# Moving weight sums from TensorE to loops on VectorE in a decode layer, with w1 loaded first

## The chip, the cores and the metric

The kernel runs on one core of a Trainium2 chip. The metric is device time in microseconds (us) for one execution; smaller is better. The core has five engines that matter here: PE (TensorE, with its weight loads listed apart as PEld), DVE (VectorE), ACT (ScalarE), POOL (GpSimd) and SP (SyncE). Each engine runs its own instruction list in order and waits on semaphores for the others. SP issues nearly all transfers from HBM to the on-chip memory; 16 DMA engines carry them.

## The reference, cut to what matters

One token of width 512 passes through a layer norm, then through two parallel branches, and all is added up. Everything is 32-bit floating point.

```python
xn = _layernorm(x)                       # x: 512 numbers, eps 1e-5
q  = (xn @ wq)                           # wq: 512 x 4096, 32 query heads of 128
# 8 key/value heads, 65536 cached keys each; 4 query heads share one of them
scores = q . k * 128**-0.5
o  = softmax(scores) . v                 # 32 heads of 128
h  = max(xn @ w1, 0)                     # w1: 512 x 1792
y  = x + o.reshape(4096) @ wo + h @ w2   # wo: 4096 x 512, w2: 1792 x 512
```

The caches k and v are 256 MiB each. The four weights are 8 MiB (wq), 8 MiB (wo), 3.5 MiB (w1) and 3.5 MiB (w2).

## The kernel before, in words

Keys are taken in 32 steps (8 key/value heads, 4 steps each). A step loads 8 MiB of k into the buffer `ks` and 8 MiB of v into the buffer `vs`; each buffer is 64 KiB deep on all 128 partitions, so it holds 32 *slices* of 512 numbers per partition, and a slice is 256 KiB in all. There is one buffer of each kind, with no second copy. In the text a slice always means these 256 KiB; wq and wo are 32 slices each, w1 and w2 are 14 each.

Queue of transfers. SP issues, in this order: wq in two pieces of 4 and 28 slices into `vs` (`WQ`, L169), the first k load into `ks` (L170); then, once PE has read all of wq (L310), the first v load. After that the loop at L312 alternates: a v load when `v_free` says that the step before has used its v, a k load when `k_free` says that the scores have been formed from the old k. At the end come w1 and w2 into `ks` (L318, L319, after the last `k_free`) and wo in seven pieces into `vs` (`WO`, L321, after the last `v_free`).

Start. DVE and PE form the layer norm with two small matmuls (L202 to L222), spread xn out (L226 to L256), and PE multiplies wq slice by slice into four rows of PSUM (L277 to L285). DVE and PE turn the result around into `qall` (L287 to L289). POOL copies the current head's query to `qcur` (L328).

A step. PE forms the scores from `ks` (L344), DVE transposes them into `tr` (L376), the maximum is found with help of PE (L349 to L351), ACT takes the exponentials (L422), and PE multiplies with `vs` into `acc_o` (L360). DVE then adds the step to `acc` (L400 or L402) and with that frees `vs` (L398). After four steps DVE closes the head (L406 to L415) into `fin`, and POOL copies it into `fins` (L332, L334).

End. PE forms xn @ w1 (L443), DVE and PE turn it around (L460, L271, L469), the heads are turned around and spread out (L453 to L494, result `sw`). PE multiplies the 14 slices of w2 and the first 28 of wo into `acc_z` (L505, helper `gather`), DVE copies that row (L536), and PE adds it together with the last four slices of wo into `acc_y` (L525, L540). DVE transposes `acc_y` (L552), and SP writes y (L561).

The helper class `Flow` counts an engine's operations on one semaphore and emits a wait only where it was not waited for already. `nc.Fori(0, n, engines=[...])` is a loop that runs on the chip: the engines named hold a counter in a register, and each turn ends with an add and a branch on each of these engines. `bass.ds(t * D, D)` is a part of a buffer whose place depends on that counter.

Of the kernel before, what the change touches and what calls it, by code (L numbers as in the profile page):

```python
# [15 lines left out]
P = 128  # L16
# [9 lines left out]
CHUNK = SK  # L26
# [3 lines left out]
NP = TPC // NT  # L30
# [6 lines left out]
WQ = [4, 28]  # L37
WO = [8, 8, 8, 4, 2, 1, 1]
PAIRED = 16
DIRECT = 28  # L40
# [29 lines left out]
def attention_and_mlp_kernel(  # L70
# [35 lines left out]
    def bank(name, *shape):  # L106
        return nc.alloc_psum_tensor(name, [P, *shape], F32).ap()

    ks = place("ks", NT * KEYS)
    vs = place("vs", NT * KEYS)  # L110
    tr = place("tr", NT * SUB, 32)
    wt = place("wt", NT * SUB, G)
    xT, xc, sq, xn = (place(n, A) for n in ("xT", "xc", "sq", "xn"))
    x4, yt = place("x4", P), place("yt", 32, 4)
    sw = place("sw", SLICES)
    mine = place("mine", HKV)
    octet = place("octet", P)
    eighth = place("eighth", R)

    flat_tr = tr.rearrange("p b i -> p (b i)")  # L120
    xs = flat_tr[:, : SLICES * HKV].rearrange("p (i h) -> p i h", h=HKV)
    xm = flat_tr[:, SLICES * HKV : SLICES * (HKV + 1)]
    om, spread = flat_tr[:, : R * HQ], flat_tr[:, R * HQ : 2 * R * HQ].rearrange("p (r h g) -> p r h g", r=R, h=HKV)
    heads = flat_tr[:, 2 * R * HQ : 2 * R * HQ + 2 * DH]
    st = place("st", 8)
# [4 lines left out]
    qall, qcur = place("qall", HKV, G), place("qcur", 32)  # L130
# [7 lines left out]
    acc, masked = place("acc", WIDE, DH), place("masked", WIDE, DH)  # L138
    fin, fins = place("fin", DH + G), place("fins", HKV, DH + G)
    rows = place("rows", 512)  # L140
    total, oT, hT = place("total", HQ), place("oT", HQ), place("hT", 4 * CT)
# [4 lines left out]
    names = "k_in v_in tiles scores m_out bias_out a_out w_out o_out k_free v_free q_in d_out f_out f_free"  # L146
    (
        k_in, v_in, s_tiles, s_dve, s_max, s_bias, s_alpha, s_w, s_o,
        k_free, v_free, q_in, s_diff, f_out, f_free,
    ) = (nc.alloc_semaphore(n) for n in names.split())  # L150
    PE, DV, AC, GP = (Flow(nc, e, n) for e, n in ((te, "pe"), (ve, "dve"), (se, "act"), (ge, "pool")))
# [6 lines left out]

    def load_slices(name, src, counts):
        marks = []  # L160
        for n in counts:
            cut = slice(len(marks) * D, (len(marks) + n) * D)
            marks += [load(sy, f"{name}{len(marks)}", vs[:, cut], src[:, cut])] * n
# [11 lines left out]
    make_identity_marks = []  # L175

# [3 lines left out]
    d = memset(DV, ones, 1.0)  # L180
    d = memset(DV, x4, 0.0)
    x4_free = DV.mark
    d = memset(DV, qcur, 0.0)
    for t in (acc_o, acc_z, pm):
        memset(DV, t, 0.0)
    memset(DV, acc_y[:, :P], 0.0)

# [9 lines left out]
    x4_in = None  # L197
    se.wait_ge(*x4_free)
    x4_in = load(se, "x4_in", x4[0:P:32, :], x.rearrange("(c n) -> c n", c=CT))


    DV.op(lambda e: e.reduce_sum(st[:, 0:1], xT, axis=AX.X), x_in)  # L202
    PE.op(lambda e: e.matmul(pm[:, 0:1], ones, st[:, 0:1], start=True, stop=True), DV.mark)
    DV.op(lambda e: e.tensor_scalar_mul(st[:, 1:2], pm[:, 0:1], 1.0 / D), PE.mark)
    DV.op(lambda e: e.tensor_scalar(xc, xT, st[:, 1:2], None, op0=ALU.subtract), DV.mark)
    DV.op(lambda e: e.tensor_mul(sq, xc, xc), DV.mark)
    DV.op(lambda e: e.reduce_sum(st[:, 2:3], sq, axis=AX.X), DV.mark)
    PE.op(lambda e: e.matmul(pm[:, 1:2], ones, st[:, 2:3], start=True, stop=True), DV.mark)
    DV.op(
        lambda e: e.tensor_scalar(st[:, 3:4], pm[:, 1:2], 1.0 / D, EPS, op0=ALU.mult, op1=ALU.add),  # L210
        PE.mark,
    )
# [3 lines left out]
    AC.op(lambda e: e.activation(alpha[:, 0:1], st[:, 3:4], AF.Exp))  # L216
# [5 lines left out]
    xn_in = DV.op(lambda e: e.tensor_scalar_mul(xn, xc, st[:, 7:8]), DV.mark)  # L222
# [14 lines left out]
    DV.op(lambda e: e.reduce_sum(mine, ident.rearrange("p (h i) -> p h i", h=HKV), axis=AX.X))  # L237
    DV.op(lambda e: e.reduce_sum(eighth, ident.rearrange("p (i r) -> p r i", r=R), axis=AX.X))
    DV.op(lambda e: e.reduce_sum(octet[:, : P // R], ident.rearrange("p (i r) -> p i r", r=R), axis=AX.X))
    DV.op(  # L240
        lambda e: e.tensor_copy(
            octet[:, P // R :].rearrange("p (h i) -> p h i", i=P // R),
            octet[:, : P // R].unsqueeze(1).to_broadcast([P, HKV - 1, P // R]),
        ),
        DV.mark,
    )
    DV.op(
        lambda e: e.tensor_mul(
            xm.rearrange("p (r a) -> p r a", a=A),
            eighth.unsqueeze(2).to_broadcast([P, R, A]), xn.unsqueeze(1).to_broadcast([P, R, A]),  # L250
        )
    )
    pz = pb[:, 1, :]
    PE.op(lambda e: e.matmul(pz[:, :SLICES], octet, xm, start=True, stop=True), DV.mark)
    xs_in = DV.op(
        lambda e: e.tensor_mul(  # L256
            xs, pz[:, :SLICES].unsqueeze(2).to_broadcast([P, SLICES, HKV]),
            mine.unsqueeze(1).to_broadcast([P, SLICES, HKV]),
        ),
        PE.mark,  # L260
    )
    DV.op(lambda e: e.memset(idg, 1.0))
    DV.op(lambda e: e.tensor_copy(idg[:, :G], ident[:G, :G]), DV.mark)

    pr, pt = pa[:, 0, :], pb[:, 0, :]

    def turn():

        for j in range(4):
            PE.op(  # L270
                lambda e: e.transpose(pt[:, j * P : (j + 1) * P], rows[:, j * P : (j + 1) * P], ident),  # L271
                DV.mark, made,
            )
        return pt.rearrange("p (j c l) -> p j c l", j=4, c=CT)

    cleared = DV.op(lambda e: e.memset(pr, 0.0))
    for i in range(SLICES):  # L277
        c = i % CT
        PE.op(
            lambda e: e.matmul(  # L280
                pr[32 * c : 32 * c + HKV, :], xs[:, i, :], vs[:, i * 512 : (i + 1) * 512],
                start=(i < CT), stop=(i >= SLICES - CT),
            ),
            cleared, xs_in, wq_in[i],
        )  # L285
    wq_read = PE.mark
    DV.op(lambda e: e.tensor_copy(rows, pr), PE.mark)  # L287
    q = turn()[:, :, :, :HKV].rearrange("p j c h -> p h j c")
    DV.op(lambda e: e.reduce_sum(qall, q, axis=AX.X), PE.mark)  # L289
    q_made = DV.mark  # L290
    PE.need(DV.mark)
    AC.need(DV.mark)


    def k_load(h, n):
        sy.wait_ge(k_free, 1).then_inc(k_free, -1)
        sy.dma_start(ks, k[h, 0, :, n * NT * KEYS : (n + 1) * NT * KEYS]).then_inc(k_in, 16)

    def v_load(h, n):
        sy.wait_ge(v_free, 1).then_inc(v_free, -1)  # L300
        src = v[h].rearrange("(p t b) d -> p t (b d)", p=P, b=SUB)
        sy.dma_start(vs, src[:, n * NT : (n + 1) * NT, :].rearrange("p t f -> p (t f)")).then_inc(v_in, 16)

    def head(h):
        v_load(h, 0)
        for n in range(1, NP):
            k_load(h, n)
            v_load(h, n)

    sy.wait_ge(*wq_read)  # L310
# [6 lines left out]
    t1, t2 = ks[:, : A * DFF], ks[:, A * DFF : A * DFF + FB * D]  # L317
# [7 lines left out]
    for h in range(HKV):  # L325
        if h:
            ge.wait_ge(f_out, h)
        ge.tensor_copy(qcur[:, :G], qall[:, h, :]).then_inc(q_in, NP)  # L328
        if h == 0:
            ge.sem_inc(f_free, 1)  # L330
        else:
            ge.tensor_copy(fins[:, h - 1, :], fin).then_inc(f_free, 1)  # L332
    ge.wait_ge(f_out, HKV)
    GP.op(lambda e: e.tensor_copy(fins[:, HKV - 1, :], fin))  # L334


    with nc.Fori(0, STEPS, engines=[ENG.PE]):
# [20 lines left out]
        for i in range(n):  # L358
            c = i % CT
            mm = te.matmul(  # L360
                acc_o[32 * c : 32 * c + WIDE * G, :],
                wt[:, i * WIDE : (i + 1) * WIDE, :].rearrange("p b g -> p (b g)"),
                vs[:, i * 512 : (i + 1) * 512],
                start=(i < CT), stop=(i >= n - CT),
            )
# [52 lines left out]
    with nc.Fori(0, HKV, engines=[ENG.Activation]):  # L418
# [16 lines left out]
        ).then_inc(s_alpha, 1)  # L435


    w = t1.rearrange("p (a f) -> p a f", a=A)
    for a in range(A):
        for c in range(CT):  # L440
            lo, hi = 512 * c, min(DFF, 512 * (c + 1))
# [151 lines left out]
```

## Time and profile before

| what | value |
|---|---|
| median of 3 runs | 1303.16 us (1303.08 to 1303.2) |
| profiled execution, own time | 1303.26 us |
| its span, first to last instruction | 1301.9 us |
| moved from HBM | 560.99 MB, 431 GB/s over the span |
| DMA engines busy with the SP queue | 99.7% |
| PE, DVE, ACT, POOL busy | 664.9, 268.4, 76.0, 4.1 us |
| mean granted TensorE clock | 0.733 |

The profile lists instructions by source line, engine and operation, with destination and sources by the program's names. A timeline row begins with the start in us from the span's start and the duration in us. "Idle before" with a releaser tells how long the engine stood before an instruction and which engine's work, or which transfer, ended that. An engine's name with a q (SPq, DVEq) is its sequencer: DMA issues, register steps, branches, waits and drains, which don't count as busy. A row of the DMA section has the size of one transfer and the time from its issue to its landing.

### The profile page before, as it was taken

Reading aid. Unit: us, or ns where it says so; the run is one execution under the profiler, and the core shown is the slowest. Engines: PE = TensorE matmul, PEld = TensorE weight load, DVE = VectorE, ACT = ScalarE, POOL = GpSimd, SP = SyncE. Lnnn points to the kernel's source line nnn. Section 1 sums busy time; section 2 is a strip of 40 time slices with the busy share of each in tenths; the row PEclk is TensorE's granted clock in tenths of the full one; section 3 lists DMA queues with packets and bytes.
Section 4 is the critical chain, followed back from the end, with each engine's and each line's share of the span. In section 5 each row is a group of like instructions: output and inputs, shape, how many; then the busy total and the mean of one; then the engine's idle time right before and its main releaser. Section 6 shows DMA issues by size and latency. Waiting matters only on the chain. (4 is left out here: it accounts for less than half of the span.)

```text
span 1301.9 us, 10665 instructions
## 1 busy us (share of the span) xinstructions
PE 664.9 (51%) x4512; PEld 185.6 (14%) x4512; DVE 268.4 (21%) x398; ACT 76.0 (6%) x292; POOL 4.1 (0%) x22
## 2 busy tenths in 40 slices
PE   3355356455446445545545545544544644544658
PEld 1111111111111111111111111111111111111112
DVE  2221122221122222012222012222112222201222
ACT  0000000000000000000000000000000000000000
POOL 0000000000000000000000000000000000000000
PEclk9776676777677677667677677768777767767769
DMA  9999999999999999999999999999999999999998
GB/s 419 419 449 419 451 419 445 425 427 443 421 449 421 449 419 451 419 445 425 431 439 425 445 421 449 419 451 419 445 425 435 435 425 445 421 449 421 449 416 361
DMA packets 11101, 561.06 MB, mean 431 GB/s; under 512 B 1492, under 2 KB 1496, under 8 KB 1880
## 3 DMA queue, kind: packets, MB, share of 16 engines
q1 hardware_dynamic: 10944, 561.00, 99.7%
q8 instruction: 3, 0.05, 0.0%
q10 hardware_dynamic: 152, 0.00, 0.0%
q14 instruction: 2, 0.02, 0.0%
HBM read 560.99 MB, written 0.00 MB: 431 GB/s over the span
## 5 line engine op out<-in xcount | busy, mean ns | idle before, releaser
L360 PE MATMUL acc_o<-vs,wt 128*16 128x512 f32 x2048 | 296.3, 743 | 179.0 <-PEq L356 179.0
L344 PE MATMUL pa<-ks,qcur 128*32 128x512 f32 x1024 | 176.5, 822 | 323.8 <-PEq L339 323.8
L376 DVE STREAM_TRANSPOSE tr<-pa 128x1024 f32<-128x1024 f32 x64 | 80.0, 1250 | 412.9 <-PE pa L344 412.9
L344 PE MATMUL pb<-ks,qcur 128*32 128x512 f32 x1024 | 139.5, 665 | 0.0
L422 ACT ACTIVATE wt<-tr,bias 128x128 f32<-128x128 f32 x128 | 64.3, 511 | 1084.5 <-ACTq L420 1084.5
L360 PEld LDWEIGHTS acc_o<-vs,wt 128*16 128x16 f32 x2048 | 69.6, 114 | 379.0 <-issue 379.0
L344 PEld LDWEIGHTS pa<-ks,qcur 128*32 128x32 f32 x1024 | 38.9, 134 | 431.4 <-issue 422.4
L402 DVE SCALAR_TENSOR_TENSOR acc<-acc,alpha,acc_o 128x512 f32<-128x512 f32 x24 | 17.9, 747 | 353.2 <-PE acc_o L360 353.2
L376 DVE STREAM_TRANSPOSE tr<-pb 128x1024 f32<-128x1024 f32 x64 | 80.0, 1250 | 49.6 <-PE pb L344 49.6
L344 PEld LDWEIGHTS pb<-ks,qcur 128*32 128x32 f32 x1024 | 41.9, 132 | 107.8 <-issue 88.6
L349 PE MATMUL pm<-ident,m 128*4 128x128 f32 x32 | 10.3, 320 | 87.7 <-DVE m L388 67.2
L400 DVE COPY acc<-acc_o 128x512 f32<-128x512 f32 x8 | 5.5, 692 | 121.5 <-PE acc_o L360 121.5
L350 PE MATMUL pm<-dg,ones 4*128 4x4 f32 x64 | 15.4, 309 | 21.4 <-DVE dg L392 21.4
L385 DVE TENSOR_REDUCE mc<-tr 128x4 f32<-128x512 f32 x24 | 24.1, 1006 | 1.8
L422 ACT ACTIVATION_READ_ACCUMULATOR wt<-tr,bias 128x1 f32 x128 | 23.9, 187 | 0.0
L349 PEld LDWEIGHTS pm<-ident,m 128*4 128x4 f32 x32 | 2.6, 81 | 116.7 <-DVE m L388 89.0
L350 PEld LDWEIGHTS pm<-dg,ones 4*128 4x128 f32 x64 | 12.6, 245 | 29.0 <-DVE dg L392 29.0
L351 PE MATMUL pm<-dg,rowg 4*128 4x1 f32 x64 | 14.7, 296 | 0.0
L280 PE MATMUL pa<-vs,tr 128*8 128x512 f32 x64 | 9.6, 754 | 8.7 <-DMA vs<-wq 7.4
L351 PEld LDWEIGHTS pm<-dg,rowg 4*128 4x128 f32 x64 | 13.4, 258 | 0.0
L390 DVE TENSOR_REDUCE mg<-pm 4x1 f32<-4x128 f32 x32 | 8.9, 279 | 13.2 <-PE pm L349 13.2
L505 PE MATMUL acc_z<-vs,sw 128*1 128x512 f32 x56 | 10.1, 592 | 2.1 <-DMA vs<-wo 2.1
(98 smaller groups left out, 97.8 us busy)
## 6 DMA issues: line engine op xcount, KB each, us to landing
vs<-wq SPq DMA_DIRECT2D x1, 7168.0 KB, 21.3
ks<-w SPq DMA_DIRECT2D x2, 3584.0 KB, 22.4
vs<-wo SPq DMA_DIRECT2D x3, 2048.0 KB, 16.4
vs<-wq SPq DMA_DIRECT2D x1, 1024.0 KB, 4.8
vs<-wo SPq DMA_DIRECT2D x1, 1024.0 KB, 22.8
ks<-k SPq DMA_DIRECT2D x32, 28.8
vs<-v SPq DMA_DIRECT2D x32, 28.9
vs<-wo SPq DMA_DIRECT2D x1, 512.0 KB, 23.6
```

What stands on the lines that cost most here:

```text
L280: lambda e: e.matmul(pr[32 * c : 32 * c + HKV, :], xs[:, i, :], vs[:, i * 512 : (i + 1) * 512], start=(i < CT), stop=(i >= SLICES - CT),),
L344: i = te.matmul(tile_of[32 * c : 32 * c + 32, :], qcur, ks[:, at : at + TW], start=True, stop=True)
L349: te.transpose(pm[:G, :P], m, ident)._wait_ge(s_dve, 3).then_inc(s_max, 1)
L350: te.matmul(pm[:, P : P + G], ones[:G, :], dg[:, :G], start=True, stop=True)._wait_ge(s_dve, 4)
L351: te.matmul(pm[:, P + G : P + G + 1], rowg, dg[:, G : G + 1], start=True, stop=True).then_inc(s_max, 1)
L360: mm = te.matmul(acc_o[32 * c : 32 * c + WIDE * G, :], wt[:, i * WIDE : (i + 1) * WIDE, :].rearrange("p b g -> p (b g)"), vs[:, i * 512 : ...
L376: i = ve.transpose(tr[:, s * SUB : (s + 2) * SUB, :].rearrange("p b i -> p (b i)"), (pa, pb)[s // 2 % 2].rearrange("p i k -> p (i k)"),)._ ...
L385: i = ve.reduce_max(top, tr[:, :, :G].rearrange("p b g -> p g b"), axis=AX.X)
L390: ve.reduce_max(mg, pm[:G, :P], axis=AX.X)._wait_ge(s_max, 1)
L402: ve.scalar_tensor_tensor(flat, flat, alpha[:, n : n + 1], acc_o, op0=ALU.mult, op1=ALU.add)
L422: i = se.activation(wt[:, :, g], tr[:, :, g], AF.Exp, bias=bias[:, n, g : g + 1], scale=scale, accum_out=part[:, n, g : g + 1],)
L505: lambda e: e.matmul(acc_z[32 * c : 32 * c + 1, :], lhsT, row, start=c not in begun, stop=last),
```

## The change

Setup. The buffers `ks` and `vs` become halves of one buffer `kv`. x is loaded as 16 rows of 32 numbers, once instead of twice; the layer norm's two sums are formed on DVE with 32x32 transposes in place of two matmuls. SP issues w1 first, into `ks`, with a rearranged source: "(i h) a f -> h i (a f)", 8 groups of 16 rows, for the 128 partitions. wq follows in two halves of 16 slices. The first k load waits until DVE has read w1 (`w1_read`); the first v load waits for all 32 adds over wq (`q_dve`).

w1. DVE multiplies and adds its 4 pieces of 1792 (128 partitions each) into `h1`, PE sums over the partitions with 4 matmuls, DVE turns the result into 14 columns of `hs` and takes the maximum with 0. This lies ahead of wq's sum.

wq. A loop on DVE of 32 turns: each waits for its slice (`go_dve`, raised by POOL in two lots of 16), adds slice times a column of `xs` onto `accq`, and drains. One matmul and four small transposes then make the queries.

Main loop. As before, but the loops of DVE, ACT and POOL become one `Fori` over heads, SP's runs over steps, PE's branch gets a prefetch hint, and DVE's loop loses its `head_slot`. The arrays k and v are cut so that each load is one contiguous 8 MiB. The last v load goes in two pieces (21 and 11 slices), and PE waits for the second before its 22nd group.

End. w2 (two halves of 7 slices) and the first 16 slices of wo go into `ks` after the last `k_free`, the other 16 of wo after the last `v_free`. Over the first 34 of these 46 slices runs a loop of 17 turns: ACT scales an even slice in place and PE adds it up with a column of ones, DVE adds the odd slice onto `accy` and drains. Five further slices DVE adds alone, four go through PE to `acc_z`, DVE adds both sums into `rows`, and PE takes `rows` and the last three slices into `acc_y`. Transpose and store are as before, without the small loop around the transpose. TensorE's instruction list shrinks from 812 to 446.

```diff
-WQ = [4, 28]
-WO = [8, 8, 8, 4, 2, 1, 1]
-PAIRED = 16
-DIRECT = 28
+WO = [9, 7, 5, 4, 4, 1, 1, 1]
+DIRECT = 29
+LATE = 21 * D
+TURNS = 17
+ALONE = 5
...
-        x_in = load(se, "x_in", xT, x.rearrange("(p a) -> p a", p=P))
-        wq_in = load_slices("wq", wq.rearrange("h (i r) a f -> (h i) (r a f)", r=R), WQ)
-        sy.dma_start(ks, k[0, 0, :, : NT * KEYS]).then_inc(k_in, 16)
+        x_in = load(se, "x_in", x16, x.rearrange("(i s) -> i s", s=32))
+        w1_in = load(sy, "w1_in", t1, w1.rearrange("(i h) a f -> h i (a f)", h=HKV))
+        wq_in = load_slices("wq", vs, wq.rearrange("h (i r) a f -> (h i) (r a f)", r=R), [SLICES // 2, SLICES // 2])
...
+    for a in range(A):
+        w = t1[:, a * DFF : (a + 1) * DFF]
+        if a == 0:
+            DV.op(lambda e: e.tensor_scalar_mul(h1, w, xn[:, 0:1]), DV.mark, w1_in)
+        else:
+            DV.op(
+                lambda e: e.scalar_tensor_tensor(h1, w, xn[:, a : a + 1], h1, op0=ALU.mult, op1=ALU.add), DV.mark
+            )
+    w1_read = DV.mark
...
+    for n in range(2):
+        ge.wait_ge(*wq_in[n * SLICES // 2]).then_inc(go_dve, SLICES // 2)
+    DV.need(xs_in, hid_in, blank)
+    with nc.Fori(0, SLICES, engines=[ENG.DVE]) as t:
+        ve.wait_ge(go_dve, 1).then_inc(go_dve, -1)
+        ve.scalar_tensor_tensor(
+            accq, vs[:, bass.ds(t * D, D)], xs[:, bass.ds(t, 1)], accq, op0=ALU.mult, op1=ALU.add
+        ).then_inc(q_dve, 1)
+        ve.drain()
...
+    sy.wait_ge(*w1_read)
+    sy.sem_inc(v_late, 16 * (STEPS - 1))
+    sy.dma_start(ks, k_parts[0]).then_inc(k_in, 16)
+    sy.wait_ge(q_dve, SLICES)
     sy.sem_inc(v_free, 1)
-    with nc.Fori(0, HKV - 1, engines=[ENG.SP]) as h:
-        head(h)
-        k_load(h + 1, 0)
-    head(HKV - 1)
+    with nc.Fori(0, STEPS - 1, engines=[ENG.SP]) as i:
+        v_load(i)
+        k_load(i + 1)
+    sy.wait_ge(v_free, 1).then_inc(v_free, -1)
+    sy.dma_start(vs[:, :LATE], v_parts[STEPS - 1][:, :LATE]).then_inc(v_in, 16)
+    sy.dma_start(vs[:, LATE:], v_parts[STEPS - 1][:, LATE:]).then_inc(v_late, 16)
     sy.wait_ge(k_free, 1)
-    w1_in = load(sy, "w1_in", t1, w1.rearrange("p a f -> p (a f)"))
-    w2_in = load(sy, "w2_in", t2, w2.rearrange("p j n -> p (j n)"))
+    w2_in = load_slices("w2", t2, w2.rearrange("p j n -> p (j n)"), [FB // 2, FB // 2])
+    near = [n for i, n in enumerate(WO) if FB + sum(WO[: i + 1]) <= SLICES]
+    wo_in = load_slices("wo", wos, wo_of, near)
     sy.wait_ge(v_free, 1)
-    wo_in = load_slices("wo", wo.rearrange("h (i r) g f -> (h i) (r g f)", r=R), WO)
+    wo_in += load_slices("wo", wos, wo_of, WO[len(near) :], at=sum(near))
...
+    with nc.Fori(0, TURNS, engines=[ENG.Activation, ENG.PE, ENG.DVE]) as t:
+        even, odd = (kv[:, bass.ds((t * 2 + i) * D, D)] for i in range(2))
+        se.wait_ge(go_act, 1).then_inc(go_act, -1)
+        se.activation(even, even, AF.Copy, scale=hs[:, bass.ds(t * 2, 1)]).then_inc(go_pe, 1)
+        te.wait_ge(go_pe, 1).then_inc(go_pe, -1)
+        te.matmul(acc_z[:1], ones[:, 0:1], even, start=False, stop=False)
+        ve.wait_ge(go_dve, 1).then_inc(go_dve, -1)
+        ve.scalar_tensor_tensor(accy, odd, hs[:, bass.ds(t * 2 + 1, 1)], accy, op0=ALU.mult, op1=ALU.add)
+        ve.drain()
+    for j in range(gathered - CT, gathered):
+        c = (j + 1) % CT
+        PE.op(
+            lambda e: e.matmul(
+                acc_z[32 * c : 32 * c + 1], hs[:, j : j + 1], kv[:, j * D : (j + 1) * D], start=(c != 0), stop=True
+            ),
+            arrivals[j], sw_in,
+        )
+    z_in = PE.mark
+    for j in range(TURNS * 2, TURNS * 2 + ALONE):
+        ve.wait_ge(go_dve, j - TURNS * 2 + 1)
+        DV.op(
+            lambda e: e.scalar_tensor_tensor(
+                accy, kv[:, j * D : (j + 1) * D], hs[:, j : j + 1], accy, op0=ALU.mult, op1=ALU.add
+            ),
+            DV.mark,
+        )
+    folded = DV.op(lambda e: e.tensor_add(rows, accy, acc_z), z_in, DV.mark)
...
+    for j in range(DIRECT, SLICES):
+        if j == SLICES - 1:
+            direct(ones[:, 0:1], rows, folded)
+        direct(
+            hs[:, FB + j : FB + j + 1], wos[:, j * D : (j + 1) * D], sw_in, wo_in[j],
+            first=(j == DIRECT), last=(j == SLICES - 1),
+        )
```

More of the change, by code (lines that the diff above doesn't have):

```diff
@@ L29 @@
 NT = 8
-NP = TPC // NT
+NP = NCH
 STEPS = HKV * NP
@@ L207, in attention_and_mlp_kernel @@
[L207 to L212, printed above, removed]
+    memset(GP, accq, 0.0)
+    memset(GP, qall, 0.0)
+    memset(GP, accy, 0.0)
+    blank = GP.mark
+    memset(DV, ones, 1.0)
+    memset(DV, qcur, 0.0)
+    memset(DV, pm, 0.0)
+    half = R * 2
@@ new lines, in attention_and_mlp_kernel @@
+    for c in range(CT):
+        PE.op(
+            lambda e: e.matmul(pm[32 * c : 32 * c + 1, : 32 * FB], ones[:, 0:1], mlp[:, c], start=True, stop=True),
+            w1_read,
+        )
+    mlp_in = PE.mark
+    xs_in = DV.op(lambda e: e.tensor_copy(xs, x_of))
+    DV.op(lambda e: e.transpose(turned, pm[:, : 32 * FB]), mlp_in)
+    DV.op(
+        lambda e: e.tensor_scalar_max(hs[:, :FB], turned.rearrange("p (j l) -> p j l", l=32)[:, :, 0], 0.0), DV.mark
+    )
+    DV.op(
+        lambda e: e.tensor_mul(
+            rows[:half].rearrange("i (j s) -> i j s", s=32), x16.unsqueeze(1).to_broadcast([half, half, 32]),
+            ident[:half, :half].unsqueeze(2).to_broadcast([half, half, 32]),
+        ),
+    )
@@ new lines, in attention_and_mlp_kernel @@
+    for t in (acc_o, acc_z):
+        memset(DV, t, 0.0)
+    memset(DV, acc_y[:, :P], 0.0)
+    hid_in = DV.mark
+    for n in range(2):
[7 more added lines that the diff above has]
+        ve.drain()
@@ L333, in attention_and_mlp_kernel @@
[L333 to L337 removed]
+    ge.sem_inc(f_free, 1)
+    ge.tensor_copy(qcur[:, :G], qall[:, 0, :]).then_inc(q_in, NP)
+    with nc.Fori(0, STEPS, engines=[ENG.PE], hint_back_edge=True):
         te.wait_ge(k_in, 16).then_inc(k_in, -16)
@@ new lines, in attention_and_mlp_kernel, with direct @@
+    folded = DV.op(lambda e: e.tensor_add(rows, accy, acc_z), z_in, DV.mark)
+    def direct(lhsT, row, *marks, first=False, last=False):
+        for c in range(CT):
+            PE.op(
+                lambda e: e.matmul(
+                    acc_y[32 * c : 32 * c + 1, :P], lhsT, row[:, c * P : (c + 1) * P], start=first, stop=last
+                ),
+                *marks,
+            )
+    for j in range(DIRECT, SLICES):
[4 more added lines that the diff above has]
+            first=(j == DIRECT), last=(j == SLICES - 1),
+        )
@@ L492, in attention_and_mlp_kernel @@
     )
-    sw_in = DV.op(
-        lambda e: e.reduce_sum(
-            sw.rearrange("p (r g) -> p r g", r=R), spread.rearrange("p r h g -> p r g h"), axis=AX.X
-        ),
-        DV.mark,
-    )
-    begun = set()
-    def gather(c, lhsT, row, marks, last=False):
-        PE.op(
-            lambda e: e.matmul(acc_z[32 * c : 32 * c + 1, :], lhsT, row, start=c not in begun, stop=last),
-            *marks,
-        )
-        begun.add(c)
-    for c in range(CT):
-        own = slice(32 * c, 32 * c + 1)
-        PE.op(
-            lambda e, own=own: e.matmul(acc_y[own, :P], ones[own, 0:1], x4[own], start=True, stop=False),
-            x4_in,
-        )
```

340 lines of the change are left out of this document (134 added, 206 removed).

## The prediction

> **What bounds the kernel now.** I read the page's slices and DMA section first, then the timeline of both ends, then the groups.
>
> ```profile
> span 1301.9 us, 10665 instructions
> DMA  9999999999999999999999999999999999999998
> q1 hardware_dynamic: 10944, 561.00, 99.7%
> q8 instruction: 3, 0.05, 0.0%
> q10 hardware_dynamic: 152, 0.00, 0.0%
> vs<-wq SPq DMA_DIRECT2D x1, 7168.0 KB, 21.3
> vs<-wq SPq DMA_DIRECT2D x1, 1024.0 KB, 4.8
> vs<-v SPq DMA_DIRECT2D x32, 28.9
> ```
>
> The 16 DMA engines are busy from end to end with SP's queue. The time is the start of the first transfer, 561 MB at a fixed rate, and a short end. Nothing saves more than the two ends; anything that leaves the queue empty costs in full. The two wq rows give the pace: issued at 0.97 and 0.43 later (next fence), 4 slices land at 5.8 and 28 more at 22.7, so 16.9 / 28 = 0.604 us per slice, 19.3 us per 8 MiB. A transfer on an idle queue lands 4.8 - 4 x 0.604 = 2.4 us after its issue, plus its own length. In the steady state a v load lands 28.9 us after its issue, of which 19.3 is its own: each is issued 28.9 - 19.3 - 2.4 = 7 us before the queue would run dry. That is all the cover.
>
> ```profile
> 0.97 0.86 SPq L155 DMA_DIRECT2D vs<-wq  x2
> 13.49 1.89 PE L280 MATMUL pa<-vs,tr 128*8 128x512 f32 x8 [1.32 <-DVE pa L276]
> 22.80 7.74 PE L280 MATMUL pa<-vs,tr 128*8 128x512 f32 x56 [7.42 <-DMA vs<-wq]
> 31.11 0.35 SPq L302 DMA_DIRECT2D vs<-v  x1
> 42.51 2.79 PE L344 MATMUL pa<-ks,qcur 128*32 128x512 f32 x12 [10.42 <-PEq L339]
> ```
>
> At the start PE is done with wq at 22.80 + 7.74 = 30.5 and SP issues the first v load at 31.1 (0.57 later), while the first k load streams until about 42.3, where PE starts on it. So PE's sum over wq hides by 9 us.
>
> **The change, part by part.** *Start: w1 first.* w1's 14 slices move from the end to the start. In bytes this is neutral; the first k load would land at 42.3 + 14 x 0.604 = 50.8, and the first v load must be issued by 50.8 - 2.4 = 48.4 or the queue runs dry. On all 16 engines w1 lands at 1.0 + 2.4 + 8.5 = 11.9. But its source steps 8 groups of 16 rows, and no load of before does that. The nearest row is the ACT queue's 152 packets: the 128-row x load makes 128 + 16 completions, so the second one, of 4 rows, made only 8, 4 rows and 4 completions: it ran on 4 engines. If the outermost count sets the engines, w1 runs on 8, takes 17 us and lands at 20.3. Bounds 11.9 and 20.3; I take 20.3, as the row is for a small count too. [...]
>
> *DVE ahead of wq.* The layer norm stays under w1's transfer: before, it and the spreading of xn were over at 13.49, where PE starts on wq.
>
> ```profile
> L402 DVE SCALAR_TENSOR_TENSOR acc<-acc,alpha,acc_o 128x512 f32<-128x512 f32 x24 | 17.9, 747 | 353.2 <-PE acc_o L360 353.2
> L400 DVE COPY acc<-acc_o 128x512 f32<-128x512 f32 x8 | 5.5, 692 | 121.5 <-PE acc_o L360 121.5
> L409 DVE TENSOR_TENSOR masked<-acc,selb 128x512 f32<-128x512 f32 x8 | 5.5, 686 | 0.0
> L463 DVE COPY tr<-pb 128x256 f32<-128x256 f32 x1 | 0.4, 424 | 0.2 <-PE pm L458 0.2
> L376 DVE STREAM_TRANSPOSE tr<-pa 128x1024 f32<-128x1024 f32 x64 | 80.0, 1250 | 412.9 <-PE pa L344 412.9
> L178 DVE MEMSET acc_o<- 128x512 f32 x1 | 0.5, 485 | 0.1
> ```
>
> An element costs (692 - 424) / 256 = 1.05 ns, and 686 from on-chip memory beside 692 from PSUM says that the source hardly matters. So a multiply-add of 512 is 0.747, of 1792 it is 2.09; four are 8.4, and w1 is read at 28.7. Then four narrow matmuls (8 cold passes, 1.9), a transpose of 448 (0.7 between 0.41 and 1.25), a maximum (0.2), a 512-wide product (0.69) and three memsets (1.15): the wq loop starts at 33.4. SP's k load, behind `w1_read`, goes out at 29, before wq is through.
>
> *The wq loop.* The drain makes its turn serial.
>
> ```profile
> L406 DVEq DRAIN  x8: 650/652/652, 188.5 to 1273.0; - x8
> L370 DVEq COMPARE_BRANCH  x9: 100/129/143, 32.3 to 1274.8; - x9
> L370 DVEq ALU_OP  x8: 45/45/58, 190.2 to 1274.7; - x8
> L398 DVEq EVENT_SEMAPHORE  x32: 21/21/21, 72.2 to 1272.8; - x32
> L302 SPq FUSED_REGOPS  x7: 37/37/42, 30.9 to 962.8; - x7
> 1272.92 0.75 DVE L402 SCALAR_TENSOR_TENSOR acc<-acc,alpha,acc_o 128x512 f32<-128x512 f32 x1 [15.54 <-PE acc_o L360]
> 1273.74 0.17 DVE L408 TENSOR_TENSOR diff<-bias 128x12 f32<-128x12 f32 x1
> ```
>
> The L406 drain, issued behind the add at 1272.92, stands until the add is over: it lasts 0.65, and the next work starts at 1273.74, 0.07 after the add's end. Only then come counter (0.045), branch (0.129), the address steps that `bass.ds` needs (0.037 each on SP, one or two), the wait (0.021), and about 0.1 from the wait (1272.8) to the add (1272.92). Recorded durations alone: 0.747 + 0.07 + 0.045 + 0.129 + 0.021 + 0.1 = 1.11 per turn, the lower bound. The sequencer's own gaps (counter at 1274.7, branch at 1274.8: near 0.09 per step) bring six steps to 0.53: 1.35, which I take; 0.11 per step gives 1.5. So 32 turns take 43.2 (35.5 to 48), the last add ends at 33.4 + 43.2 - 0.5 = 76.1, SP issues v at 76.7. Late by 76.7 - 48.4 = **28.3 us** (20.8 to 33.0; 8.4 less if w1 has 16 engines). The queue has nothing else: the next k load stands behind this v load on SP and needs the scores, which need the queries. Behind it the old 7 us of cover return, since the step's work is unchanged.
>
> *The main loop.* Merged loops, the branch hint and the contiguous loads I cost at nothing, hidden by those 7 us; each load still has 128 rows of 64 KiB. Without that cover they would cost their control, some 0.3 us per step.
>
> *The end.* All in us before or after E, the landing of the last wo slice.
>
> ```profile
> 1243.69 3.64 PE L344 MATMUL pa<-ks,qcur 128*32 128x512 f32 x16 [10.78 <-PEq L339]
> 1259.41 0.19 ACT L422 ACTIVATION_READ_ACCUMULATOR wt<-tr,bias 128x1 f32 x1
> 1263.04 9.70 PE L360 MATMUL acc_o<-vs,wt 128*16 128x512 f32 x64 [5.86 <-PEq L356]
> 1274.77 1.06 DVE L415 TENSOR_REDUCE fin<-masked 128x128 f32<-128x512 f32 x1
> 1275.88 0.29 POOL L334 COPY fins<-fin 128x132 f32<-128x132 f32 x1 [155.46 <-DVE fin L415]
> 1276.23 0.62 PE L453 MATMUL pb<-fins,selg 128*4 128x256 f32 x8
> 1277.57 0.35 DVE L468 RECIPROCAL total<-pm 128x32 f32<-128x32 f32 x1
> 1299.15 0.78 PE L540 MATMUL acc_y<-vs,sw 128*1 128x128 f32 x16
> 1299.52 0.11 PEld L540 LDWEIGHTS acc_y<-vs,sw 128*1 128x1 f32 x8 [0.27 <-DMA vs<-wo]
> 1300.07 0.41 DVE L552 STREAM_TRANSPOSE yt<-acc_y 128x128 f32<-128x128 f32 x1 [1.19 <-PE acc_y L540]
> 1300.51 0.34 SPq L155 DMA_DIRECT2D y<-yt  x1
> ```
>
> Before, E is 1299.5 and the span ends 2.4 later. After, 46 slices follow the last v load, not 60: it lands at E - 27.8, the last k at E - 47.1. Scores to exponentials take 1259.6 - 1243.7 = 15.9 (E - 31.2); the 9.7 of `acc_o` then run to E - 21.5 (its 22nd group comes at E - 24.8, so the split load holds nothing up). DVE closes the head in 3.1 (E - 18.4), POOL's two copies 0.5, PE's heads 1.1, and DVE's five small steps 1.8 (transpose of 256 near 0.5, reciprocal 0.35, three of 0.25): the loop over w2 and wo starts at E - 15.0. DVE has 17 turns of the same form, 23.0: E + 8.0. Five lone adds at 0.80 (no loop, but each waits for the last): E + 12.0. One add (0.75), 16 short passes and hand-over (0.8), and the old 2.0 from there to the span's end: E + 15.6 against E + 2.4, **13.2 us** (9.1 at 1.11, 15.7 at 1.5). The slices arrive at 1.21 per pair, ahead of DVE throughout. ACT (no drain) and PE keep pace.
>
> *TensorE's shorter program.* Instruction blocks come over the same engines.
>
> ```profile
> q8 instruction: 1, 0.02, 2.4%
> ...
> 1297.00:1298.00 1.00, 1.00 (x8) 0.10 (x8) 0.00 (x0) 0.00 (x0) 0.00 (x0) 1.00 0.59 211
> 1298.00:1299.00 1.00, 0.73 (x24) 0.38 (x24) 0.69 (x1) 0.00 (x0) 0.00 (x0) 1.00 0.14 55
> ```
>
> One block, between 46 and 48.5, took 2.4% of 16 x 2.5 us: 0.96 us of one engine. At the end (last column but one, DMA share) most engines finish near 1297.7, a few at 1299: laggards of up to 1.2 us. Fewer blocks save 0 to 1.2; I take 0.6.
>
> **Sum.** 1303.26 (the profiled execution, 0.1 above the median of 1303.16, within the noise) + 28.3 + 13.2 - 0.6 = 1344 us. Own range 1324 to 1352.
>
> **Rivals.** *Control hidden:* if counter, branch and wait run under the add in spite of the drain, a turn is 0.78. The wq loop is over at 58.5, v is late by 10.7, the end by 3.8: 1317. For it: semaphore steps like L405 do run under an add. Against: the 0.65 drain. *Block fetches:* if a short loop straddles two instruction blocks and fetches one each turn, 49 turns gain 1 us or more each: 1393 and up. Against: PE's loop turned 32 times with three fetches in all. [...] *Not slower:* the adds run at the memset's 0.485 with control beneath, and w1 uses 16 engines. Then 32 turns from 25.0 end with wq's arrival at 31, v is in time, the end waits for data: 1302.7. It decides at (48.4 - 0.6 - 25.0) / 32 = 0.71 per turn. For it: only that a memset of 512 is faster than a copy; against: 686 for a product from on-chip memory.
>
> **How the numbers follow.** Serial turns 0.82 (with 8 engines 0.57, 16 engines 0.25), control hidden 0.10, fetches 0.05, not slower 0.03. The time is that of the likeliest. From 1317, to take in the second, to 1354 the range holds about 0.8, as the serial case may miss its bounds too. What a measurement tells from no change is 0.2%, 2.6 us: of the last case most is within it, the rest slower.
>
> **What would show it.** w1's first multiply at 20 (or 12); DVE adds 1.35 apart from 33 to 76; SP's first v issue near 77, with an empty DMA stretch of 10 to 25 us ahead; the main loop as before; after the last slice lands, 17 spaced adds still running and y 15 us later. Wrong if adds come under 1.1 apart, if v goes out before 48, or if DVE's loops are stretched by q8 or q14 rows.

## The result, and the profile after

The changed kernel takes 1382.73 us (median of 5 runs, 1381.44 to 1383.43) against 1303.2 us before (1303.08 to 1303.46): 1.0608 times as long, 95% interval 1.0596 to 1.062. The direction was forecast, the size was not: 1344 was predicted, the range ended at 1354.

The page of the changed kernel, its span, the DMA share in 40 slices of the span, and the two queues that the prediction spoke of:

```profile
span 1382.1 us, 11154 instructions
DMA  9947999999999999999999999999999999999993
q1 hardware_dynamic: 11368, 561.00, 96.3%
q8 instruction: 1, 0.02, 0.0%
```

The same 561 MB are moved, but the queue isn't full at the start (third and fourth slice) and the last slice is a third full. The slice row doesn't show the larger loss. That needs the rates by stage (columns: window, its length, busy time of PE, PEld, DVE, ACT and POOL, granted clock, DMA share, GB/s):

```profile
3.00:20.00 17.00, 0.63 (x2) 0.50 (x2) 5.61 (x26) 2.97 (x4) 1.73 (x6) 1.00 1.01 151
20.00:50.00 30.00, 0.00 (x0) 0.00 (x0) 0.00 (x0) 0.00 (x0) 0.00 (x0) 1.00 1.02 151
50.00:61.00 11.00, 0.66 (x4) 0.10 (x8) 7.51 (x5) 0.00 (x0) 0.00 (x0) 1.00 0.59 238
61.00:82.00 21.00, 2.87 (x10) 0.08 (x2) 11.54 (x18) 0.00 (x0) 0.00 (x0) 1.00 1.00 424
82.00:90.00 8.00, 0.00 (x0) 0.00 (x0) 4.14 (x6) 0.00 (x0) 0.00 (x0) 1.00 0.45 197
90.00:112.00 22.00, 1.60 (x2) 0.10 (x2) 10.89 (x15) 0.00 (x0) 0.00 (x0) 1.00 0.09 30
112.00:1350.00 1238.00, 635.65 (x4276) 178.43 (x4276) 260.72 (x369) 78.05 (x296) 3.63 (x17) 0.72 1.00 433
```

From 3 to 50 us the engines count as fully busy, and move 151 GB/s. Before, the first fortieth of the span had 419. A share of 1.00 says that every engine has a packet under way, not how fast it advances. From 90 on the queue is empty until v goes out at 110.8 (the 30 GB/s of that row are v's first bytes), and from 112 on the main loop runs at 433 GB/s.

The timeline of the changed kernel shows what follows from that at the start (SP's issues and some of DVE's rows):

```profile
0.97 0.77 SPq L164 DMA_DIRECT2D kv<-w  x1
1.80 0.88 SPq L164 DMA_DIRECT2D kv<-wq  x2
52.77 1.15 DVE L258 TENSOR_SCALAR tr<-kv,xn 128x1792 f32<-128x1792 f32 x1 [41.56 <-DMA kv<-w]
53.96 6.32 DVE L261 SCALAR_TENSOR_TENSOR tr<-kv,xn,tr 128x1792 f32<-128x1792 f32 x3
60.38 0.33 SPq L337 DMA_DIRECT2D kv<-k  x1
65.34 0.75 DVE L293 SCALAR_TENSOR_TENSOR acc<-kv,xs,acc 128x512 f32<-128x512 f32 x1 [0.47 <-DVEq L292]
66.80 0.75 DVE L293 SCALAR_TENSOR_TENSOR acc<-kv,xs,acc 128x512 f32<-128x512 f32 x1 [0.71 <-DVEq L292]
...
109.59 0.75 DVE L293 SCALAR_TENSOR_TENSOR acc<-kv,xs,acc 128x512 f32<-128x512 f32 x1 [0.68 <-DVEq L292]
110.80 0.35 SPq L333 DMA_DIRECT2D kv<-v  x1
```

DVE waits 41.56 us for w1 and multiplies first at 52.77. The adds over wq run from 65.34 to 110.34, and the first v load goes out at 110.80: 62.4 us after the 48.4 at which the queue would have stayed full.

And at the end:

```profile
1348.06 0.75 DVE L509 SCALAR_TENSOR_TENSOR accy<-kv,hs,accy 128x512 f32<-128x512 f32 x1 [0.32 <-DVEq L508]
1349.55 0.75 DVE L509 SCALAR_TENSOR_TENSOR accy<-kv,hs,accy 128x512 f32<-128x512 f32 x1 [0.74 <-DVEq L508]
...
1371.76 0.75 DVE L509 SCALAR_TENSOR_TENSOR accy<-kv,hs,accy 128x512 f32<-128x512 f32 x1 [0.73 <-DVEq L508]
1372.82 4.18 DVE L523 SCALAR_TENSOR_TENSOR accy<-kv,hs,accy 128x512 f32<-128x512 f32 x5 [0.32 <-issue]
1377.11 0.69 DVE L528 TENSOR_TENSOR rows<-accy,acc_z 128x512 f32<-128x512 f32 x1
1379.47 0.35 SPq L164 DMA_DIRECT2D y<-yt  x1
```

The last bytes of wo move in the stretch from 1360 to 1362 (two windows of the same view):

```profile
1360.00:1362.00 2.00, 2.00 (x9) 0.44 (x11) 1.27 (x2) 0.00 (x0) 0.00 (x0) 1.00 0.37 135
1362.00:1363.00 1.00, 1.00 (x16) 0.19 (x8) 0.27 (x2) 0.00 (x0) 0.00 (x0) 1.00 0.01 2
```

With the 0.4 us from the last byte to the release that stood there before (bytes until 1299.0 or so, release at 1299.52), E is about 1362.5 and the span ends at E + 19.6, where it ended at E + 2.4: 17.2 us. The two ends together, 62.4 + 17.2 = 79.6, on 1303.26 make 1382.9; the profiled execution took 1383.43.

### The profile page after: what moved, and what is told of

The parts are those of the page before. It is cut to its first block, busy times and chain, and to the rows that moved or that the text cites. A ratio compares the mean times of both kernels' runs of the same rounds, so it can differ in the third digit from the quotient of the medians.

```text
span 1382.1 us, 11154 instructions
## 1 busy us (share of the span) xinstructions
PE 656.6 (48%) x4358; PEld 182.5 (13%) x4358; DVE 316.8 (23%) x460; ACT 87.5 (6%) x309; POOL 5.6 (0%) x27
## 5 line engine op out<-in xcount | busy, mean ns | idle before, releaser
L383 PE MATMUL acc_o<-kv,wt 128*16 128x512 f32 x2048 | 296.2, 743 | 173.3 <-PEq L377 173.3
L365 PE MATMUL pa<-kv,qcur 128*32 128x512 f32 x1024 | 176.3, 821 | 315.3 <-PEq L360 315.3
L365 PE MATMUL pb<-kv,qcur 128*32 128x512 f32 x1024 | 140.6, 669 | 0.0
L383 PEld LDWEIGHTS acc_o<-kv,wt 128*16 128x16 f32 x2048 | 69.9, 114 | 372.9 <-issue 372.9
L365 PEld LDWEIGHTS pa<-kv,qcur 128*32 128x32 f32 x1024 | 39.0, 134 | 422.9 <-issue 414.3
L365 PEld LDWEIGHTS pb<-kv,qcur 128*32 128x32 f32 x1024 | 42.2, 132 | 108.1 <-issue 89.0
L293 DVE SCALAR_TENSOR_TENSOR acc<-kv,xs,acc 128x512 f32<-128x512 f32 x32 | 24.1, 752 | 21.4 <-DVEq L292 21.4
L507 PE MATMUL acc_z<-kv,ones 128*1 x34 | 16.7, 653 | 0.0
L371 PEld LDWEIGHTS pm<-dg,ones 4*128 4x128 f32 x64 | 12.6, 245 | 29.0 <-DVE dg L436 29.0
L509 DVE SCALAR_TENSOR_TENSOR accy<-kv,hs,accy 128x512 f32<-128x512 f32 x17 | 12.8, 751 | 12.0 <-DVEq L508 11.3
## 6 DMA issues: line engine op xcount, KB each, us to landing
kv<-w SPq DMA_DIRECT2D x2, 1792.0 KB, 15.6
```

The lines of the kernel that those rows point to most:

```text
L293: ve.scalar_tensor_tensor(accq, vs[:, bass.ds(t * D, D)], xs[:, bass.ds(t, 1)], accq, op0=ALU.mult, op1=ALU.add).then_inc(q_dve, 1)
L365: i = te.matmul(tile_of[32 * c : 32 * c + 32, :], qcur, ks[:, at : at + TW], start=True, stop=True)
L371: te.matmul(pm[:, P : P + G], ones[:G, :], dg[:, :G], start=True, stop=True)._wait_ge(s_dve, 4)
L383: mm = te.matmul(acc_o[32 * c : 32 * c + WIDE * G, :], wt[:, i * WIDE : (i + 1) * WIDE, :].rearrange("p b g -> p (b g)"), vs[:, i * 512 : ...
L507: te.matmul(acc_z[:1], ones[:, 0:1], even, start=False, stop=False)
L509: ve.scalar_tensor_tensor(accy, odd, hs[:, bass.ds(t * 2 + 1, 1)], accy, op0=ALU.mult, op1=ALU.add)
```

## The experiments

Two questions were open: why w1 came at 52 and not at 20 us, and what a turn of DVE's loops is made of. Where the source of w1 is laid out otherwise, the host has put its rows in that order. A time with a range behind it is a median, with the interval of its ratio to the kernel before, which took 1303.4 to 1303.5 us beside them; a time without one is a single execution.

### w1 in plain rows

The same rows arrive in the same partitions, but from an array that has them in that order, so the load is one of 128 whole rows.

```diff
-        w1_in = load(sy, "w1_in", t1, w1.rearrange("(i h) a f -> h i (a f)", h=HKV))
+        w1_in = load(sy, "w1_in", t1, w1.rearrange("p a f -> p (a f)"))
```

> w1 is laid out on the host in the order in which the changed kernel puts it on the partitions, so that its load is 128 plain rows and nothing else changes. The theory: what was mis-sized in the prediction is w1's landing (first use at 52.8 us where 20.3 was taken), because the load runs on 8 engines and slows everything beside it. Then the first multiply on w1 comes near 12 us, the first v load goes out near 70 instead of 110.8, and the time falls by about 41 us to 1342. Rival: w1 is late because being first in the queue costs it (a cold start of the memory); then it stays near 50 and the time near 1382.

Measured 1342.56 us (1341.29 to 1343.18), ratio 1.0297 (1.028 to 1.0315). Its first stage by windows, and the rows of its timeline that answer to those above:

```profile
3.00:20.00 17.00, 0.68 (x6) 0.55 (x10) 13.12 (x31) 2.97 (x4) 1.73 (x6) 1.00 0.99 426
```

```profile
12.37 1.15 DVE L258 TENSOR_SCALAR tr<-kv,xn 128x1792 f32<-128x1792 f32 x1 [1.52 <-DMA kv<-w]
70.41 0.34 SPq L333 DMA_DIRECT2D kv<-v  x1
```

Half of the change's whole loss, 40 of 79.5 us, is the form of this one load. That the result is so near the 1344 predicted is chance: the prediction had assumed 8 engines and w1 at 20.3; here it has 16 and comes at 12.4, and longer turns and a longer end make up for the difference.

### Eight groups, but of neighbouring rows in the source

Against the idea that the strided source is slow: 8 groups of 16 rows, each group contiguous, with one unused row behind each so that the groups stay apart.

```diff
+        w1_in = load(sy, "w1_in", t1, w1[:, :16].rearrange("g i a f -> g i (a f)"))
```

> w1 is laid out on the host as 8 groups of 16 rows with one row of zeros behind each group (not loaded), so the load still steps 8 groups of 16 rows and puts the same rows on the same partitions, but each group is now one contiguous stretch. Destination theory (8 engines, each writing 16 neighbouring partitions, collide where they write): nothing changes, w1 near 52 us and 1382. Source theory (8 engines reading 8 neighbouring rows at once collide where they read): w1 lands near 20, the plain half rate, and the time is about 1350.

Measured 1383.35 us, first multiply at 53.05. The first two windows, where the strided source had 151 and 151 GB/s:

```profile
3.00:20.00 17.00, 0.63 (x2) 0.49 (x2) 5.61 (x26) 2.97 (x4) 1.72 (x6) 1.00 0.99 148
20.00:50.00 30.00, 0.00 (x0) 0.00 (x0) 0.00 (x0) 0.00 (x0) 0.00 (x0) 1.00 1.03 153
```

The stride of the source plays no part here.

### Sixteen groups of eight rows

> w1 laid out on the host as 16 groups of 8 rows with a row of zeros behind each (not loaded): the load steps 16 groups of 8 rows and each group goes to 8 neighbouring partitions. If the number of groups sets the engines, 16 run. If only the number of engines matters: w1 near 12 us and a time near 1342, as with plain rows. If it also matters which partitions an engine writes: the packets of w1 take more than the 1.07 us of a plain 28 KB row, w1 lands at 17 to 35, and the time is 1347 to 1365.

Measured 1352.71 us. The edit is the line above with `w1[:, :8]`, on an array that the host has cut into 16 groups.

```profile
3.00:20.00 17.00, 0.63 (x2) 0.49 (x2) 5.62 (x26) 2.97 (x4) 1.73 (x6) 1.00 0.98 210
```

```profile
21.47 1.15 DVE L258 TENSOR_SCALAR tr<-kv,xn 128x1792 f32<-128x1792 f32 x1 [10.21 <-DMA kv<-w]
```

The first is the window of the first stage, the second the timeline's row of w1's first multiply. All 16 engines are at work, and move half of the 426 GB/s of plain rows. So the number of engines isn't the whole matter: 16 groups of 8 rows in place of 128 plain rows cost half the rate at the same share (0.98 and 0.99).

### w1 with nothing beside it

SP waits for w1 before it issues wq, with the load as in the changed kernel.

```diff
         w1_in = load(sy, "w1_in", t1, w1.rearrange("(i h) a f -> h i (a f)", h=HKV))
+        sy.wait_ge(*w1_in)
```

> The changed kernel, but SP waits for w1 before it issues wq, so that the 8-group load runs with no other transfer beside it. Company theory (8 engines on w1 and 8 on wq slow each other): w1 alone lands near 20, its first multiply comes there, and the time is about 1350 to 1355. If w1 is slow by itself: first multiply still at 40 to 52, wq's halves 12 and 22 us later, and the time about 1375 to 1385.

Measured 1376.05 us. SP issues wq at 37.45, when w1 has landed; two windows before that:

```profile
3.00:20.00 17.00, 0.00 (x0) 0.00 (x0) 0.00 (x0) 0.00 (x0) 0.00 (x0) 1.00 0.50 110
20.00:36.00 16.00, 0.00 (x0) 0.00 (x0) 0.00 (x0) 0.00 (x0) 0.00 (x0) 1.00 0.47 100
```

A share of a half is 8 engines, and they move about 105 GB/s, a quarter of the 426 of plain rows, where half of the engines at the same pace would move half. By the trace's packet records one packet of w1 (28 KB, a row) takes 2.19 us here, 1.06 in plain rows, and 3.19 in the changed kernel, where wq runs beside it (all these are medians; no packet record names its engine, but a share of 0.5 alone and 1.0 with wq says that wq ran on the other 8: at 10, 20, 30 and 40 us of the changed kernel 8 packets of each are under way). wq's 32-KB packets take 3.6 as long as w1 runs and 1.21 otherwise. So both: by itself the load is at half pace, and in company it and its company fall to a third. (The wait stands in the opening section, whose end all engines await, so the layer norm too starts only at 39.5 and the first multiply comes at 46.87; the time of this kernel holds that.)

### The same 8 engines, other partitions

w1 in four loads of 32 partitions, each in 8 groups of 4 rows. If each group goes to one engine, which no record shows, an engine then writes 4 neighbouring partitions of each quarter in place of 16 neighbours.

```diff
+        w1_in = nc.alloc_semaphore("w1_in"), 16 * CT
+        for c in range(CT):
+            sy.dma_start(t1[32 * c : 32 * (c + 1)], w1[c, :, :4].rearrange("e i a f -> e i (a f)")).then_inc(w1_in[0], 16)
```

> [...] Theory (which partitions the 8 engines write at one time is what costs; with 16 neighbours each they get in one another's way, with 4 they do not): w1's first multiply at 20 to 28 us, its packets near 1.1 us apiece as long as wq does not run into them and at most 2.2, and the time 8 to 16 us above the kernel with w1 in plain rows (1342.6): 1350 to 1359 us. Rival (8 engines on a source in groups are slow wherever they write): w1's first multiply near 52 us and 1383 us as before.

Measured 1358.74 us, within the theory's range and far from 1383; the first multiply came at 31.03, later than the 28 allowed, and v at 89.07. And the same with SP waiting for w1 before wq:

> The four spread loads of w1, and SP issues wq only when w1 has landed: nothing else runs beside w1. Theory (8 engines at full pace when none writes where another does): w1's packets of 28 KB take 1.07 us each, as in plain rows, 16 of them per engine, and the first multiply comes at 19.5 to 21 us, which is the 20.3 that the prediction took; with neighbouring partitions and nothing beside it was 37. The wq loop then starts near 33, held at most a little by wq's landing, v goes out near 79 and the time is 1350 to 1354 us. Rival (groups cost by themselves): first multiply at 30 or later and 1362 us or more.

The window of the first stage, and the timeline's row in which SP issues wq:

```profile
3.00:20.00 17.00, 0.00 (x0) 0.00 (x0) 0.00 (x0) 0.00 (x0) 0.00 (x0) 1.00 0.48 207
```

```profile
20.79 0.84 SPq L164 DMA_DIRECT2D kv<-wq  x2
```

Again 8 engines (0.48), but 207 GB/s where neighbours gave 110 and 100: w1 has landed at 20.8, a packet takes 1.06 us. That is the 20.3 of the prediction, met by 8 engines in this form, with nothing beside them. The first multiply came at 30.20 and not at 20, which had been named as the rival's sign, and the time was 1360.77 us, above the 1354 that the theory allowed and below the rival's 1362: I had overlooked that the wait holds up the layer norm here as well (DVE's first row is at 22.8). So it is w1's landing and its packets that decide for the theory, not the multiply or the time. In company, without that wait, w1's packets are at 1.1 first and 2.25 towards the end, 273 GB/s from 3 to 36 us.

Together these runs leave one reading for this load: what made it slow by itself is which partitions its engines write at one time. It is an estimate from the packet times and not shown itself, since the records name neither the engine of a packet nor the partition that it writes. A packet of 28 KB took 2.19 us in 8 groups of 16 neighbours (alone), 2.24 in 16 groups of 8, and 1.06 in 8 groups of 4 per quarter (alone), against 1.06 in plain rows. Two things are not kept apart from that: the spread form is also four loads and not one, and it reads other places of the source; against them stand that a single load of plain rows is fast (426 GB/s) and one in 16 groups slow (210), and that the source's order made no difference above (1383.35 us). How the partitions would bring this about, no trace here shows. Nor does a run here tell why wq's packets beside it slow from 1.21 to 3.6 us, though by the shares they are on other engines.

### wq's loop written out, with its drain

From here on all kernels have w1 in plain rows. First only the loop goes: 32 pieces with fixed addresses, the wait and the drain of each kept.

```diff
-    with nc.Fori(0, SLICES, engines=[ENG.DVE]) as t:
+    for t in range(SLICES):
         ve.wait_ge(go_dve, 1).then_inc(go_dve, -1)
         ve.scalar_tensor_tensor(
-            accq, vs[:, bass.ds(t * D, D)], xs[:, bass.ds(t, 1)], accq, op0=ALU.mult, op1=ALU.add
+            accq, vs[:, t * D : (t + 1) * D], xs[:, t : t + 1], accq, op0=ALU.mult, op1=ALU.add
         ).then_inc(q_dve, 1)
         ve.drain()
```

> w1 in plain rows, and wq's loop written out as 32 pieces, with the drain and the wait of each add kept: only counter, branch and address steps are gone. By the split of the prediction (add 0.747, drain 0.07, wait 0.02, hand-over 0.1; the rest are loop steps) an add comes every 0.94 to 1.0 us in place of 1.43: 32 x 0.45 = 14 us less, v goes out at 56 and the time is 1328 us. Rival (the drain is what makes the turn long): an add still every 1.35 to 1.43 us and 1340 to 1342 us.

Measured 1327.54 us, v at 55.79. Three rows of its timeline:

```profile
33.56 0.75 DVE L293 SCALAR_TENSOR_TENSOR acc<-kv,xs,acc 128x512 f32<-128x512 f32 x1 [0.20 <-DVEq L292]
34.52 0.75 DVE L293 SCALAR_TENSOR_TENSOR acc<-kv,xs,acc 128x512 f32<-128x512 f32 x1 [0.20 <-DVEq L292]
35.48 0.75 DVE L293 SCALAR_TENSOR_TENSOR acc<-kv,xs,acc 128x512 f32<-128x512 f32 x1 [0.20 <-DVEq L292]
```

An add every 0.96 us in place of 1.427 ((109.59 - 65.34) / 31). Counter, branch and address steps are 0.47 of a turn, drain and wait 0.2.

### wq's loop written out, without the drain

The wait on a counter that POOL raises goes too: each add waits for the one before, and DVE itself waits for the two halves of wq (those lines aren't shown).

```diff
-        ve.wait_ge(go_dve, 1).then_inc(go_dve, -1)
+        ve.wait_ge(q_dve, t)
...
-        ve.drain()
```

> w1 in plain rows, wq's loop written out, and each add waits for the one before by a semaphore, without drain, counter, branch or address steps. An add every 0.80 us, as the lone adds at the end show: 32 x 0.63 = 20 us less than 1342.6, v goes out at 50.4 and is late by 2: 1322.5 us. What is left over 1303.3 is then the end alone, 17.2, and 2. If the start holds something else that costs (the longer instruction list of VectorE, say), it is more than 1326.

Measured 1320.87 us (1320.56 to 1321.15), ratio 1.0134 (1.0117 to 1.0151), v at 50.49. The 32 adds stand in one row of the timeline, 25.23 us, 0.79 each:

```profile
24.81 25.23 DVE L293 SCALAR_TENSOR_TENSOR acc<-kv,xs,acc 128x512 f32<-128x512 f32 x32
```

So drain and counted wait cost 0.17 more per add than a wait on the add's own semaphore. The edit exchanges both, but the counted wait stands with only 0.021 in the record, so most of it is the drain. v is 2.1 late, and the 15.3 us that remain over the kernel before are the end. That is 1.9 less than in the changed kernel and why the time came out under the 1322.5 expected: the first add at the end stands 16.2 us before the last bytes (1285.45 and 1301.7) where it stood 14.0 before them (1348.06 and 1362.1). Why the bytes come later here, no run tells.

### The end's adds written out too

DVE's 17 adds leave the loop, which ACT and PE keep.

```diff
-        ve.wait_ge(go_dve, 1).then_inc(go_dve, -1)
-        ve.scalar_tensor_tensor(accy, odd, hs[:, bass.ds(t * 2 + 1, 1)], accy, op0=ALU.mult, op1=ALU.add)
-        ve.drain()
+    for j in range(1, TURNS * 2, 2):
+        DV.op(
+            lambda e: e.scalar_tensor_tensor(
+                accy, kv[:, j * D : (j + 1) * D], hs[:, j : j + 1], accy, op0=ALU.mult, op1=ALU.add
+            ),
+            DV.mark, arrivals[j],
+        )
```

> As the last, and DVE's share of the loop at the end written out too (ACT and PE keep theirs). DVE's 17 adds over w2 and wo come every 0.80 us or as the slices arrive (every 1.21 for two) in place of every 1.48, so 17 x 0.68 = 11.5 us less: the span ends about 8 us after the last slice lands in place of 19.6, and the time is 1311 us. If the end is held up by ACT and PE, by the arrivals or by the chain behind the loop, it stays above 1316.

Measured 1310.3 us (1309.12 to 1310.92), ratio 1.0049 (1.0033 to 1.0066). The end of DVE's timeline:

```profile
1287.21 13.35 DVE L506 SCALAR_TENSOR_TENSOR accy<-kv,hs,accy 128x512 f32<-128x512 f32 x17
1300.59 3.90 DVE L522 SCALAR_TENSOR_TENSOR accy<-kv,hs,accy 128x512 f32<-128x512 f32 x5
1304.60 0.69 DVE L527 TENSOR_TENSOR rows<-accy,acc_z 128x512 f32<-128x512 f32 x1
```

The 22 adds now follow one another without a gap, and still end 3 us after the last bytes (1301.4 by the packet records): DVE starts on them 14 us before that, and 22 times 0.79 is 17.3. Its share is too large even without any control.

### The end's sums back on TensorE

The loop of 17 turns and the five lone adds go, and in their place stands:

```diff
+    for j in range(gathered):
+        c = (j + 1) % CT
+        PE.op(
+            lambda e: e.matmul(
+                acc_z[32 * c : 32 * c + 1], hs[:, j : j + 1], kv[:, j * D : (j + 1) * D],
+                start=(c != 0 and j < CT), stop=(j >= gathered - CT),
+            ),
+            hid_in, arrivals[j], *([sw_in] if j >= FB else []),
+        )
```

> w1 in plain rows, wq's adds written out on DVE, and the sums at the end back on TensorE: 43 matmuls with a column of weights each, over four rows of PSUM in turn, and no share of DVE or ACT; TensorE's list grows again by about 40 instructions. If DVE's share is what makes the end long, the span ends 2.4 to 3.5 us after the last slice lands, as before the change, and the time is 1304 to 1306 us; what is then left over the kernel before is the 1.5 us by which v is late and the add into rows. If the end is long for another reason (the merged loops, the later head, the store), it stays at 8 us after the last slice and 1310 us.

Measured 1307.18 us (1306.91 to 1308.34), ratio 1.0031 (1.0019 to 1.0044), 1.2 above the range that was expected. Three rows of its timeline:

```profile
1299.56 1.04 PE L493 MATMUL acc_z<-kv,hs 128*1 128x512 f32 x8 [1.29 <-DMA kv<-wo]
1300.75 0.69 DVE L500 TENSOR_TENSOR rows<-accy,acc_z 128x512 f32<-128x512 f32 x1 [14.20 <-PE acc_z L493]
1302.69 0.34 SPq L164 DMA_DIRECT2D y<-yt  x1
```

PE waits for wo again, as before the change, and the sum is over when the last slices land. Of the 3.8 us that remain over 1303.4, 1.6 is the late v (50.02 against 48.4), and 1.6 is the store of y, which took 3.0 us from issue to landing where it took 1.4 before. The latter isn't explained: the same store took 1.6 in both kernels with the spread loads of w1, 2.6 in the changed one, and 2.1 to 3.0 in the rest (one profiled execution of each). No version here beats the kernel before. That one keeps the DMA queue full from end to end (99.7%) and is over 2.4 us after the last byte's release, so a change at the two ends has almost nothing to win there.

## Why the prediction was wrong, and where it was right

**The step that failed is the price of w1's load**, "takes 17 us and lands at 20.3", with its "Bounds 11.9 and 20.3". w1's first multiply came at 52.77, 32.5 us later, and this is 32.5 of the 38.7 us by which the time was missed. The count of engines was right: 8, by the share of 0.50 with w1 alone. What failed is the sentence behind it, unspoken: that 8 engines move half of what 16 do, whatever they write. They moved a quarter (105 GB/s), and with wq beside them all 16 moved 151. Alone, w1 had landed by 37.45, 17 us later than was taken; the other 15 came from the company of wq, which the prediction put at nothing. Neither bound could hold it, because both assumed full pace per engine. The row that was used, 152 small packets, was read for a count of engines and says nothing about their pace; a load of 3.5 MiB in 8 groups had no row, and its upper bound should have said so.

**The turn was a little short.** 1.35 was taken; 1.427 was measured in wq's loop (45.0 us for 32 turns against 42.7: 2.3 more) and (1371.76 - 1348.06) / 16 = 1.48 in the loop at the end. The split behind it was right in kind: loop steps 0.47, and drain, wait and hand-over small. Written out, the adds came at 0.96, within the 0.94 to 1.0 that this split gave. Its parts were sized from other rows and came out otherwise: the address step took 0.093 where 0.037 was taken from SP, the branch 0.056 where 0.129 was taken (below, in ns: smallest, median and largest of 32).

```profile
L293 DVEq FUSED_REGOPS  x32: 93/93/99, 65.2 to 109.5; - x32
L291 DVEq COMPARE_BRANCH  x32: 50/56/56, 66.3 to 110.5; - x32
```

**From w1's first multiply to wq's first add** it takes 12.6 us, where 13.1 had been worked out (the first of the four pieces took 1.15 and not 2.09), and v leaves 0.5 after the last add. So with w1 at 52.77 the steps of the prediction alone would have given v at 109.2; it left at 110.80.

**The end was forecast at 13.2 and cost 17.2.** The loop starts at E - 14.4 (E - 15.0), its last add is over at E + 10.0 (E + 8.0), the five lone adds at E + 14.5 (E + 12.0), the span at E + 19.6 (E + 15.6). Of the 4.0 us that are missing, 0.6 is the start, 1.4 the turns, 0.5 the lone adds (0.86 apart, not 0.80), and 1.5 what follows them, of which 1.2 is the slower store of y.

**The main loop** costs nothing, as said: 433 GB/s from 112 to 1350.

**TensorE's shorter list** was put at a gain of 0.6. The block fetches on q8 fell from 3 to 1, so what was argued happened; a gain can't be seen. Both ends added to the time before give 1382.9, the profiled execution took 1383.43.

**The rivals.** *Control hidden* falls: an add every 1.43 us, and 0.47 less per turn once the loop steps are gone. *Block fetches* falls: the turns are even, 0.67 idle in each, and q8 moved one packet, q14 two, as before. *Not slower* falls with both of its conditions. Of the list of what would show it, w1's first multiply came at 52.77 in place of 20, the DVE adds from 33 to 76 stood at 65 to 110, the empty stretch came (21 us), and when the last slice had landed the spaced adds were still running, with 7 of the 17 to go. None of the rivals was the one that happened: a load that is slow by its form was not among them.

The six terms of the miss: 32.47 (w1), -0.53 (up to wq's loop), 2.30 (its turns), -0.14 (the issue of v), 4.0 (the end), 0.6 (the list): 38.7. They are read from the profiled execution, which took 1383.43 us, 39.3 more than the sum; 0.6 of that lies in neither end.

## What to carry to other kernels

A load whose outermost count is small, or whose rows are grouped otherwise than in the other loads (here 105 and 210 GB/s against 426), is priced by GB/s from a row of that very form, and where there is none the upper bound is open; the DMA share doesn't help, since it read 1.0 at a third of the rate (151 of 426 GB/s). A short hardware loop on VectorE with one 512-wide add costs here 0.47 us per turn in counter, branch and addresses and 0.17 for drain and counted wait, nearly as much as the add (0.75); written out, with a wait on the add's own semaphore, an add came every 0.79. And work that is taken off an engine with slack onto one that must finish it behind the last byte is paid for, 3 us here with every add written out, however short the first engine's program becomes.

## What had not been expected of the hardware

- w1's load of 128 rows of 28 KB ran at 426 GB/s in plain rows (with the first of wq behind it), at 210 in 16 groups of 8 neighbouring partitions, at 105 in 8 groups of 16, and at 207 on the same number of engines in groups of 4 neighbours; the last two with nothing beside them.
- A load at such a pace slowed another one that by the shares ran on the other engines: wq's packets took 3.6 in place of 1.21 us until w1 had landed.
- The store of y, 2 KB, took between 1.4 and 3.0 us from issue to landing in kernels that differ only in what precedes it.
